# A fused attention and two mixture-of-experts kernel: ranks' products four turns later, last logits inside the first expert's products

## The chip, the cores and the metric

The kernel runs on one core of one Trainium2 chip. Times are device microseconds of one execution, lower is better. Three runs of the kernel before took 864.76, 865.23 and 867.83 us; their median, 865.23 us, is the time before.

## What is computed

Three stages follow each other, all in float32. First attention of 4 batches, 8 heads, 576 positions and head size 64, where half of the heads look at the last 32 positions and half at every fourth of the last 128. Its output, 2304 rows of 512 numbers, goes through a mixture of 8 experts with the two best experts per row, and that result through a second mixture with the best expert alone.

```python
x = attn_out.transpose(0, 2, 1, 3).reshape(B * S, H * D)
logits = x @ w_gate
noisy_logits = logits + np.log1p(np.exp(x @ w_noise)) * noise
top2 = np.argpartition(-noisy_logits, 2, axis=1)[:, :2]
...
h = np.maximum(x[mask] @ w1[e], 0.0)
out[mask] += top2_w[mask, k, None] * (h @ w2[e])
```

## The kernel before

**Attention in turns.** The attention works on 36 banks, nine blocks of 64 positions in each of four batches. One pass of the loop over `i` is one turn for one bank: scores of the next bank, softmax of this one, transposes of the exponentials `pe` of an older one (`t` and `q`), its product with the values (`v`), and for the oldest the transposes of its output `xo` (`x`), after which the rows go to memory. Three more passes, `i` = 36 to 38, empty the pipeline. The letters `a`, `v`, `w`, `t`, `q`, `x` and `r` are PSUM banks, one of each and two of `a`. Almost every matmul goes through the helper `in_order`, at L237, which stamps it so that TensorE runs them in the order in which the program is written; so nearly every TensorE row carries the same line.

**Products in three passes.** Experts' weights and inputs are split in a high and a low part (`whi` and `wlo`, `xh` and `xl`, `hh` and `hl`); each product is three matmuls: high by high, low by high, high by low. A first product of an expert makes hidden rows, a second product output rows. ScalarE makes `whi` (L219), `xh` (L722) and `hh` (L777), VectorE `wlo` (L220), `xl` (L723) and `hl` (L778).

**Routing in small steps.** As soon as rows of attention output are there, `logits_part` (L1024) multiplies half a batch's transposed rows `xT` by the gate, VectorE copies the result to `lgT` (L702), and `batch_logits` (L1031) sums four parts of it and starts a routing chain. A chain is a generator; `go_on` (L1068) is one tick and lets each list of chains make two steps, four from turn 30 on. `yield n` in a chain means that it rests n ticks. The chain finds the two best experts, sums the one-hots to `msum` (L480, 481), and `ranks` counts with TensorE how many earlier rows go to each expert (`r<-msum,before` and `r<-msum,onesb`). From the ranks come slots and one-hots `ohb` on VectorE, `rhs` on POOL, further `r` products, and a table `tabe` with the list of rows of each expert. `indices` (L450 to L456) turns a piece of the table into a list for gathering (`gata`), and POOL gathers the rows (`xg`, L716). Three parts of the rows go through it: nine tiles of 128 rows (batches 0 and 1), which fix the 256 rows of the first expert; four more tiles (batch 2), which fix 384 rows of the second; and the last five (batch 3). `V2PE`, 2, and `PE2V`, 1, are the ticks that a chain rests between VectorE and TensorE.

**Around the end of attention.** From turn 35 on each pass ends with eight steps of the first expert's first products (`first_products`, three matmuls a step, `E0_N` = 8, in two calls of `DC` = 4, each with a tick behind it). When the last bank is finished, `finish` (L961) gives `ready` the two halves of the last batch, and after the loop their logits are computed. Then the second products of the first expert, the first and second of the second, and so on follow. `put_rows` (L1186) adds finished rows `y` (made by ScalarE, L1215) to the result in memory from POOL's queue.

Of the kernel before, what the change touches and what calls it, by code (L numbers as in the profile page):

```python
# [42 lines left out]
A2V, V2PE, PE2V, POOL2V = 4, 2, 1, 10  # L43
# [4 lines left out]
E0_AT, E0_N, E0_M = 35, 8, 1  # L48
# [16 lines left out]
def attention_moe_moe_kernel(  # L65
# [9 lines left out]
    E, _, F = m1_w1.shape  # L75
    HH = H // 2
    T = N // P
    DC = DM // P
# [27 lines left out]
    def bank(tag):  # L106
        return banks_of[tag].tile([P, 512], F32, name=tag)
# [125 lines left out]
    ordered = [False]  # L233

    def in_order(op, *args, **kw):

        r = op(*args, **kw)  # L237
        if ordered[0]:
            tc.stamp_issue_order_token(r.ins, "blocks")
        return r  # L240


    def rtile(shape, name, dt=F32):
        return rt.tile(shape, dt, name=name)
# [214 lines left out]
    class Route:  # L459
# [14 lines left out]
        def ranks(self, oh, weights, t0, t1):  # L474
            n = t1 - t0
            m = rtile([P, n + 1, E], "msum", BF16)
            if self.K == 1:
                nc.vector.tensor_copy(m[:, :n], oh[:, 0])
            else:
                nc.vector.tensor_add(m[:, :n], oh[:, 0], oh[:, 1])  # L480
            nc.vector.memset(m[:, n:], 0.0)
            val = yield from weights
            ps = bank("r")[:, :(n + 1) * E].rearrange("p (t e) -> p t e", e=E)
            in_order(nc.tensor.matmul, ps, before, m, start=True, stop=False)
            for i in range(n):
                in_order(nc.tensor.matmul, ps[:, i + 1:], onesb, m[:, i:i + 1, :].to_broadcast([P, n - i, E]),
                         start=False, stop=(i == n - 1))
            yield PE2V
            rk = rtile([P, n + 1, E], "rk")
            if self.prev is None:  # L490
                nc.vector.tensor_copy(rk, ps)
            else:
                nc.vector.tensor_add(rk, ps, self.prev[:, None, :].to_broadcast([P, n + 1, E]))
            cnt = rt.tile([P, E], F32, name="cnt", bufs=2)
            nc.vector.tensor_copy(cnt, rk[:, n])
            yield
            return val, m, rk, cnt
# [198 lines left out]
    def logits_T(xt, lgT, n, tag):  # L696

        lg = bank(tag)[:, :n]
        for c in range(DC):
            o = c * P // DC  # L700
            in_order(nc.tensor.matmul, lg[o:o + P // DC], wg1[:, c], xt[c], start=True, stop=True)
        nc.vector.tensor_copy(lgT, lg)  # L702
# [52 lines left out]
    def mm1_steps(ws, x_, n):  # L755
        xh, xl = x_
        up = -(-n // P) * P
        pool = pools["h", up == regs1[0][1]]
        hh = pool.tile([P, FC, up], F32R, name=f"hh{up}")
        hl = pool.tile([P, FC, up], F32R, name=f"hl{up}")  # L760
        m = n - up + P
        if m <= P // 2:

            last = hl[:, :, up - P:].rearrange("p f (a t) -> p f a t", a=2)
            if m < P // 2:
                nc.gpsimd.memset(last[:, :, :, m:].bitcast(F32), 0.0)
        for f in range(FC):
            ph = next_bank("avaw")
            i = 0
            for c in range(DC):  # L770
                wc = tuple(w_[:, f * P:(f + 1) * P] for w_ in ws[c])
                for a, b_ in passes(wc, (xh[:, c], xl[:, c])):
                    in_order(nc.tensor.matmul, ph[:, :n], a, b_[:, :n], start=(i == 0), stop=(i == 3 * DC - 1))
                    i += 1
                if c < DC - 1:
                    yield
            nc.scalar.activation(hh[:, f, :n], ph[:, :n], AF.Relu)  # L777
            nc.vector.scalar_tensor_tensor(hl[:, f, :n], ph[:, :n], 0.0, hh[:, f, :n].bitcast(F32),  # L778
                                           op0=ALU.max, op1=ALU.subtract)
            yield  # L780
        if m <= P // 2:
            nc.gpsimd.tensor_copy(last[:, :, 1, :m], hh[:, :, n - m:n].bitcast(F32))
        return hh, hl
# [23 lines left out]
    with ExitStack() as actx:  # L807
# [63 lines left out]
        def banks():  # L871

            for j in range(0, NB - 1, 2):
                for half in (1, 0):
                    yield (half, j), (half, j + 1)
            yield (0, NB - 1), (1, NB - 1)
# [25 lines left out]
        def scores(bk, bk_next):  # L902

            if bk_next is not None:
                open_scores(bk_next)
            for u in range(HH // 2):
                for a in range(2):
                    product(bk, a, HH // 2 + u)
                    if bk_next is not None:
                        product(bk_next, a, u)  # L910
# [113 lines left out]
        def logits_part(b, c0, n, xT, lgT):  # L1024
            o = b % 2 * S + c0

            logits_T([xT[:, c, c0:c0 + n] for c in range(DC)], lgT[:, o:o + n], n, "v" if c0 else "x")
            if c0 + n == S:
                backs.append((b, lgT))
# [24 lines left out]
        chains, ready, backs, routed, tick = ([], []), [], [], [0], [0]  # L1054
# [17 lines left out]
        def first_products(n):  # L1072
            if "h" not in nxt:
                nxt["h"] = Steps(mm1_steps(w_1, first_x[0], regs1[0][1]))
            nxt["h"].take(n)

        all_banks = [(b, bi, blocks) for b in range(B) for bi, blocks in enumerate(banks())]
        n_bi = len(all_banks) // B
        to_t, to_v, to_f = (sum(SKEW[:i + 1]) for i in range(3))
# [9 lines left out]
        for i in range(len(all_banks) + to_f):  # L1089
            bi = i % n_bi  # L1090
            if i >= LAST_AT:
                per_turn[0] = LAST_PER_TURN
                go_on()
            if i < len(all_banks):
                queue.insert(0, bks[i])
                scores(bks[i], bks[i + 1] if i + 1 < len(bks) else None)
                softmax(bks[i])
                if len(queue) > to_t and queue[to_t]:
                    transposes(queue[to_t])
                exponentials(bks[i])  # L1100
                if i < len(WARM_1):
                    busy(WARM_1[i], last_pe[0])
            else:
                queue.insert(0, None)
            if i >= len(all_banks) and len(queue) > to_t and queue[to_t]:
                transposes(queue[to_t])
            if len(queue) > to_v and queue[to_v]:
                values(queue[to_v])
            known_lg = bool(backs)
            while ready:  # L1110
                logits_part(*ready.pop())
            if len(queue) > to_f:
                bk = queue.pop()
                if bk.bi == 0:
                    xT = ak.tile([P, DC, S], F32, name="xT")
                    if bk.b % 2 == 0:
                        lgT = ak.tile([P, 2 * S], F32, name="lgT")
                bk.xT = xT
                finish(bk)
                if bk.bi == n_bi - 1:  # L1120
                    ready += [(bk.b, S // 2, S // 2, xT, lgT), (bk.b, 0, S // 2, xT, lgT)]
                if known_lg:

                    batch_logits(*backs.pop())
                    go_on()
            if i >= E0_AT and 0 in first_x:
                for _ in range(0, E0_N, DC):
                    first_products(DC)
                    go_on()

            if i < len(all_banks):
                if bi == 0:
                    more = [[] for _ in range(n_bi)]
                    b = i // n_bi + 1
                    if b < B:
                        next_b = b
                        more[0].append(load_k(b))
                        more[1].append(load_q(b))
                for c, (half, f) in enumerate(V_AT):

                    if f == bi and i // n_bi + 1 < B:
                        more[bi] += load_v(next_b, half, c // 2)
                if i in Z_AT:
                    z0 = Z_AT.index(i) * ZROWS
                    more[bi] += zeros(z0, min(ZROWS, N + P - z0))
                if last_st[0] is None:
                    issue(more[bi])
                else:
                    with tc.issue_after(last_st[0]):
                        issue(more[bi])  # L1150
            if i == W1_AT:
                with tc.issue_after(last_st[0]):
                    w_1 = load_w(wr1, m1_w1[0], F, nc.gpsimd, 4, None, nc.gpsimd)
# [435 lines left out]
```

## Time and profile before

| | before |
|---|---|
| Median of three runs | 865.23 us |
| The profiled execution | 860.84 us |
| Its span | 858.7 us |
| TensorE busy | 819.0 us (95%) |
| VectorE busy | 446.1 us (52%) |
| ScalarE busy | 380.1 us (44%) |
| POOL busy | 229.5 us (27%) |
| Mean granted TensorE clock | 0.979 |

The profile is of one execution; its own time, 860.84 us, is its span, from the first to the last instruction, and 2.1 us around it. The clock is the share of full speed that the chip granted: 1.00 is 2.4 GHz, 0.50 is 1.2 GHz. A bracket behind a row of a timeline gives how long the engine was idle before it and which instruction ended the idle time; "issue" there stands for nothing that the profile shows.

### The profile page before, as it was taken

What the parts mean: (1) busy time and instruction counts of PE and PEld (TensorE: products, weight loads), DVE (VectorE), ACT (ScalarE), POOL (GpSimd) and SP (SyncE); (2) the same over time, 40 slices, a digit from 0 to 9 for tenths busy, and PEclk for the clock granted to TensorE, in tenths of its full rate; (3) what the DMA queues carried; (4) which work ended last, traced back from release to release, by engine and by line L of the source; (5) the groups of instructions that cost most, each with busy time, mean ns of one, the idle gap of its engine ahead of it and who ended that gap; (6) DMA issues with size and microseconds to landing.
All of it is one profiled execution on the core that took longest, in us unless ns stands there. A gap on an engine that the chain in (4) does not pass through costs nothing. (4 is left out here: it accounts for less than half of the span.)

```text
span 858.7 us, 15516 instructions
## 1 busy us (share of the span) xinstructions
PE 819.0 (95%) x5798; PEld 701.9 (82%) x5798; DVE 446.1 (52%) x1255; ACT 380.1 (44%) x991; POOL 229.5 (27%) x290
## 2 busy tenths in 40 slices
PE   8998989999999999999999998998999999999994
PEld 6666677888898998898988987877878979889882
DVE  4677876874262146433515344574565556446450
ACT  3876554514263143433525244314415466446550
POOL 6062442032222232322323223313222121121111
PEclk9999889999999999999999999999999999999997
DMA  9989454453284436542814426445434656644530
GB/s 250 281 271 344 142 154 142 124 155 70 53 288 104 118 65 204 152 133 31 272 25 152 140 47 157 121 123 142 108 135 164 211 188 202 243 146 148 197 120 17
DMA packets 71919, 131.82 MB, mean 154 GB/s; under 512 B 5689, under 2 KB 34441, under 8 KB 71456
## 3 DMA queue, kind: packets, MB, share of 16 engines
q1 hardware_dynamic: 58640, 97.27, 34.5%
q0 software_dynamic: 13200, 33.52, 16.7%
q8 instruction: 47, 0.77, 0.4%
q14 instruction: 32, 0.26, 0.1%
HBM read 106.86 MB, written 24.15 MB: 153 GB/s over the span
## 5 line engine op out<-in xcount | busy, mean ns | idle before, releaser
L220 DVE TENSOR_TENSOR wlo<-raw,whi 128x512 fp32r<-128x512 f32 x264 | 165.4, 686 | 128.1 <-ACT whi L219 127.6
L219 ACT CAST whi<-raw 128x512 fp32r<-128x512 f32 x264 | 144.2, 618 | 49.0 <-DMA raw<-in_moe_w_dram 24.6
L237 PE MATMUL a<-xh,whi 128*128 128x256 f32 (+13 forms) x376 | 116.2, 309 | 0.1
L237 PE MATMUL a<-xh,wlo 128*128 128x256 f32 (+13 forms) x376 | 114.3, 304 | 2.1 <-issue 2.1
L237 PE MATMUL a<-xl,whi 128*128 128x256 f32 (+13 forms) x376 | 114.3, 304 | 1.4 <-DVE xl L723 1.4
L237 PE MATMUL a<-whi,hl 128*128 128x512 f32 (+4 forms) x248 | 98.0, 395 | 0.0
L237 PE MATMUL a<-wlo,hh 128*128 128x512 f32 (+5 forms) x248 | 97.5, 394 | 0.0
L237 PE MATMUL a<-whi,hh 128*128 128x512 f32 (+4 forms) x240 | 95.9, 399 | 0.8 <-ACT whi L219 0.8
L1186 POOL DMA_INDIRECT x_scratch<-y,sca x30 | 47.6, 1587 | 139.1 <-ACT y L1215 80.0
L778 DVE SCALAR_TENSOR_TENSOR hl<-a,hh 128x256 fp32r<-128x256 f32 (+13 forms) x94 | 43.5, 462 | 68.0 <-ACT hh L777 67.8
L777 ACT ACTIVATE hh<-a 128x256 fp32r<-128x256 f32 (+13 forms) x94 | 39.1, 416 | 81.3 <-PE a L237 81.2
L237 PEld LDWEIGHTS a<-xl,whi 128*128 128x128 f32 x376 | 72.4, 193 | 2.3 <-DVE xl L723 1.6
L237 PEld LDWEIGHTS a<-xh,wlo 128*128 128x128 f32 x376 | 72.3, 192 | 2.4 <-issue 2.4
L237 PEld LDWEIGHTS a<-xh,whi 128*128 128x128 f32 x376 | 72.5, 193 | 1.4 <-ACT xh L722 0.5
L716 POOL DMA_INDIRECT xg<-x_nextscratch,gat x30 | 34.9, 1164 | 85.5 <-PE t L237 25.4
L237 PE MATMUL w<-xh,whi 128*128 128x256 f32 (+13 forms) x184 | 56.4, 307 | 0.0
L237 PE MATMUL w<-xh,wlo 128*128 128x256 f32 (+13 forms) x184 | 55.5, 302 | 0.0
L237 PE MATMUL w<-xl,whi 128*128 128x256 f32 (+13 forms) x184 | 55.5, 302 | 0.0
L237 PEld LDWEIGHTS a<-whi,hl 128*128 128x128 f32 (+4 forms) x248 | 45.7, 184 | 11.2
L237 PEld LDWEIGHTS a<-wlo,hh 128*128 128x128 f32 (+5 forms) x248 | 45.2, 182 | 10.7 <-DVE wlo L220 0.5
L237 PE MATMUL v<-xh,whi 128*128 128x256 f32 (+13 forms) x176 | 53.4, 304 | 0.0
L237 PE MATMUL v<-xl,whi 128*128 128x256 f32 (+13 forms) x176 | 53.1, 302 | 0.1
(413 smaller groups left out, 1774.7 us busy)
## 6 DMA issues: line engine op xcount, KB each, us to landing
raw<-in_moe_w_dram SPq DMA_DIRECT2D x60, 1024.0 KB, 5.8
raw<-in_moe_w_dram SPq DMA_DIRECT2D x32, 256.0 KB, 5.2
v<-in_v_dram SPq DMA_DIRECT2D x16, 288.0 KB, 5.8
x_scratch<-zero SPq DMA_DIRECT2D x2, 1792.0 KB, 7.4
k<-in_k_dram SPq DMA_DIRECT2D x3, 1152.0 KB, 7.6
q<-in_q_dram SPq DMA_DIRECT2D x3, 1152.0 KB, 10.0
x_nextscratch<-xo SPq DMA_DIRECT2D x20, 128.0 KB, 4.6
x_scratch<-zero SPq DMA_DIRECT2D x1, 1280.0 KB, 5.1
```

Source lines behind the costliest of these rows:

```text
L219: nc.scalar.copy(hi_, raw_)
L220: (nc.vector if i % 2 == 0 and all_on is None else eng).tensor_sub(lo_, raw_, hi_.bitcast(F32))
L237: r = op(*args, **kw)
L716: last_g[0] = nc.gpsimd.indirect_dma_start(out=xg[:m], out_offset=None, in_=src, in_offset=bass.IndirectOffsetOnAxis(ap=idx[:m], axis=0)).ins
L777: nc.scalar.activation(hh[:, f, :n], ph[:, :n], AF.Relu)
L778: nc.vector.scalar_tensor_tensor(hl[:, f, :n], ph[:, :n], 0.0, hh[:, f, :n].bitcast(F32), op0=ALU.max, op1=ALU.subtract)
L1186: nc.gpsimd.indirect_dma_start(out=dst, out_offset=bass.IndirectOffsetOnAxis(ap=idx, axis=0), in_=y, in_offset=None, compute_op=ALU.add)
```

## The change

`Route.ranks` rests four ticks (`2 * V2PE`) more before its products, in the attention part of the program alone. At the last turn (`i` = 38) the first expert's first products are no longer eight steps in a row: four steps, the logits of one half, two steps, the logits of the other half, two steps.

```diff
@@ -480,6 +480,8 @@
                 nc.vector.tensor_add(m[:, :n], oh[:, 0], oh[:, 1])
             nc.vector.memset(m[:, n:], 0.0)
             val = yield from weights
+            if ordered[0] == "attention":
+                yield 2 * V2PE
             ps = bank("r")[:, :(n + 1) * E].rearrange("p (t e) -> p t e", e=E)
             in_order(nc.tensor.matmul, ps, before, m, start=True, stop=False)
             for i in range(n):
@@ -1124,8 +1126,17 @@
                     batch_logits(*backs.pop())
                     go_on()
             if i >= E0_AT and 0 in first_x:
-                for _ in range(0, E0_N, DC):
-                    first_products(DC)
+                for g in range(0, E0_N, DC):
+                    if i + 1 < len(all_banks) + to_f:
+                        first_products(DC)
+                    elif g == 0:
+                        first_products(DC)
+                        logits_part(*ready.pop())
+                    else:
+                        first_products(DC // 2)
+                        logits_part(*ready.pop())
+                        first_products(DC // 2)
                     go_on()
 
             if i < len(all_banks):
```

Line numbers behind L482 grow by 2, behind L1128 by 11. Three places show what moves.

TensorE, the ranks' products of the second part, before (`xo` is attention output, `msum` the summed one-hots, `xh_2141` the first expert's rows):

```order
L237 MATMUL t<-ident,pe 96x128 x2
L237 MATMUL q<-ident,pe 96x128 x2
L237 MATMUL v<-v,pT 64x64 x8
L237 MATMUL x<-ident,xo 128x128 x2
L237 LDWEIGHTS before
L237 MATMUL r<-msum,before 128x40
L237 LDWEIGHTS onesb
L237 MATMUL r<-msum,onesb 128x32
```

Here they follow the transposes `x` of one bank and precede the scores of the next. Now, from the same bank on:

```order
L237 MATMUL x<-ident,xo 128x128 x2
L237 MATMUL w<-k_273,q_271 64x96 x4
L237 MATMUL t<-ident,pe 96x128 x2
L237 MATMUL q<-ident,pe 96x128 x2
L237 MATMUL v<-v,pT 64x64 x8
L237 MATMUL x<-ident,xo 128x128 x2
L237 MATMUL a<-xh_2180,whi 128x256
```

The products are gone from behind the first `x`; they stand 24 first products later:

```order
L237 MATMUL a<-xh_2180,whi 128x256
L237 MATMUL a<-xl_2181,whi 128x256
L237 MATMUL a<-xh_2180,wlo 128x256
L237 LDWEIGHTS before
L237 MATMUL r<-msum,before 128x40
L237 LDWEIGHTS onesb
L237 MATMUL r<-msum,onesb 128x32
```

The first part's products move in the same way, from ahead of a bank's `v` to behind the next bank's scores.

TensorE at the end of attention, before, where the logits of the last two halves (`xT,wg`) come behind all first products:

```order
L237 MATMUL a<-xh_2141,whi 128x256
L237 MATMUL a<-xl_2142,whi 128x256
L237 MATMUL a<-xh_2141,wlo 128x256
L237 MATMUL x<-xT,wg_243 32x288 x4
L237 MATMUL v<-xT,wg_243 32x288 x4
L237 MATMUL v<-sum_245,lgT 128x16 x5
L237 MATMUL a<-whi,hh_2434 128x512
```

And now:

```order
L237 MATMUL a<-xl_2181,whi 128x256
L237 MATMUL a<-xh_2180,wlo 128x256
L237 MATMUL x<-xT,wg_243 32x288 x4
L237 MATMUL r<-rhs,ohb 128x120 x3
L237 MATMUL a<-xh_2180,whi 128x256
L237 MATMUL a<-xl_2181,whi 128x256
L237 MATMUL a<-xh_2180,wlo 128x256
L237 MATMUL a<-xh_2180,whi 128x256
L237 MATMUL a<-xl_2181,whi 128x256
L237 MATMUL a<-xh_2180,wlo 128x256
L237 MATMUL v<-xT,wg_243 32x288 x4
```

The first half's logits stand 12 first products ahead of the end, the second half's six. The last three `rhs` products of the second part, earlier well ahead of here, now stand among them.

POOL and TensorE at the end of the second expert's second products. POOL before (`gatf` and `gat` are lists of rows, `scaa` a list for adding):

```order
L716 DMA xg<-x_nextscratch,gatf 128x512
L716 DMA xg<-x_nextscratch,gatf 72x512
L716 DMA xg<-x_nextscratch,gat 128x512
L1186 DMA x_scratch<-y,scaa_2555 2432x512
L716 DMA xg<-x_nextscratch,gat 128x512
L716 DMA xg<-x_nextscratch,gat 104x512
```

And now:

```order
L718 DMA xg<-x_nextscratch,gatf 128x512
L718 DMA xg<-x_nextscratch,gatf 72x512
L1197 DMA x_scratch<-y,scaa_2650 2432x512
L718 DMA xg<-x_nextscratch,gat 128x512 x2
L1197 DMA x_scratch<-y,scaa_2650 2432x512
L718 DMA xg<-x_nextscratch,gat 104x512
```

The scatter has moved ahead of the first `gat`. TensorE before, at the transposes of these rows:

```order
L237 MATMUL t<-ident,xg 128x128 x4
L237 MATMUL a<-whi,hh_2902 128x512
L237 MATMUL a<-wlo,hh_2902 128x512
L237 MATMUL a<-whi,hl_2903 128x512
L237 MATMUL x<-ident,xg 128x72 x4
```

And now:

```order
L237 MATMUL a<-whi,hl_2903 128x512
L237 MATMUL t<-ident,xg 128x128 x4
L237 MATMUL x<-ident,xg 128x72 x4
L237 MATMUL q<-ident,xg 128x128 x4
L237 MATMUL v<-xh_3261,whi 128x200
```

A third transposition, `q`, stands between the second products and the first products of 200 rows; before, it stood behind these.

## Rows read from the trace of the kernel before

**Rows 1.** The page: engine, busy us, share of the span, instructions.

```profile
PE 819.0 (95%) x5798; PEld 701.9 (82%) x5798; DVE 446.1 (52%) x1255; ACT 380.1 (44%) x991; POOL 229.5 (27%) x290
```

**Rows 2.** Waits of TensorE: waited for, us in total, times, longest us.

```profile
PE r L237 <- DVE msum L481: 2.2, 1, 2.2
...
PE v L237 <- DVE xo L958: 1.8, 6, 0.5
```

**Rows 3.** TensorE's timeline: start, length, line, operation, count, idle before, releaser.

```profile
90.45 0.39 PE L237 MATMUL t<-ident,pe 128*96 128x128 f32 x2 [0.79 <-DVE ai L375]
...
92.28 1.10 PE L237 MATMUL v<-v,pT 96*64 96x64 f32 x16 [1.00 <-issue]
...
105.45 0.42 PE L237 MATMUL t<-ident,pe 128*96 128x128 f32 x2
```

**Rows 4.** Stretches: length; busy PE, PEld, DVE, ACT, POOL; PEclk, DMA share, GB/s.

```profile
92.00:96.00 4.00, 3.72 (x39) 2.90 (x40) 4.00 (x15) 1.85 (x10) 2.25 (x5) 0.54 0.18 49
96.00:100.00 4.00, 3.89 (x39) 2.23 (x39) 3.64 (x15) 1.66 (x9) 1.48 (x3) 0.60 0.92 347
...
116.00:120.00 4.00, 3.86 (x37) 3.04 (x38) 3.33 (x23) 3.04 (x17) 1.43 (x6) 0.53 0.84 242
120.00:124.00 4.00, 4.00 (x24) 4.00 (x24) 2.79 (x13) 1.39 (x7) 1.77 (x4) 0.62 0.73 207
...
140.00:144.00 4.00, 3.89 (x9) 2.81 (x10) 3.85 (x7) 3.81 (x9) 0.00 (x0) 0.57 0.10 16
152.00:156.00 4.00, 2.93 (x14) 1.90 (x12) 4.00 (x9) 3.19 (x6) 0.50 (x1) 1.00 0.69 179
...
588.00:592.00 4.00, 1.41 (x10) 0.93 (x10) 4.00 (x8) 4.00 (x9) 1.38 (x1) 1.00 0.59 158
```

**Rows 5.** TensorE's timeline, ranks' products of the second part.

```profile
116.14 0.19 PE L237 MATMUL r<-msum,before 128*128 128x40 bf16 x1 [2.24 <-DVE msum L481]
```

**Rows 6.** TensorE's timeline, end of attention and the first expert.

```profile
138.04 1.29 PE L237 MATMUL v<-sum,lgT 128*128 128x16 f32 x10 [0.58 <-DVE lgT L702]
140.08 0.78 PE L237 MATMUL a<-whi,hh 128*128 128x512 f32 x1 [0.75 <-ACT whi L219]
...
156.38 0.44 PE L237 MATMUL a<-xl,whi 128*128 128x384 f32 x1 [1.38 <-DVE xl L723]
```

**Rows 7.** VectorE's timeline, 115 to 156 us.

```profile
115.88 0.19 DVE L480 TENSOR_TENSOR msum<-oh 128x32 bf16<-128x32 f32 x1
...
130.22 0.27 DVE L553 TENSOR_TENSOR tabe<-tabe,r 128x120 f32<-128x120 f32 x1
...
140.15 4.91 DVE L220 TENSOR_TENSOR wlo<-raw,whi 128x512 fp32r<-128x512 f32 x8 [0.17 <-ACT whi L219]
...
155.64 0.69 DVE L723 TENSOR_TENSOR xl<-q,xh 128x512 fp32r<-128x512 f32 x1
```

**Rows 8.** TensorE's timeline, 168 to 192 us.

```profile
168.80 0.20 PE L237 MATMUL r<-msum,before 128*128 128x48 bf16 x1
...
189.45 0.66 PE L237 MATMUL t<-ident,xg 128*128 128x128 f32 x4
...
191.64 0.26 PE L237 MATMUL v<-xh,whi 128*128 128x200 f32 x1
```

**Rows 9.** POOL's timeline, 184 to 191 us.

```profile
184.78 1.01 POOL L716 DMA_INDIRECT xg<-x_nextscratch,gatf  x1 [1.24 <-DVE tabr L657]
...
187.42 0.98 POOL L716 DMA_INDIRECT xg<-x_nextscratch,gat  x1 [0.35 <-issue]
189.10 1.62 POOL L1186 DMA_INDIRECT x_scratch<-y,scaa  x1 [0.70 <-issue]
```

**Rows 10.** Tile `xg` (gathered rows), 100 to 206 us: landing of its transfers.

```profile
DMA to landing us min/median/max: 3.3/3.8/4.6
```

**Rows 11.** ScalarE's timeline: the row that the scatter takes.

```profile
185.59 0.69 ACT L1215 ACTIVATE y<-w,wgta 128x512 f32<-128x512 f32 x1 [5.98 <-PE w L237]
```

## The prediction

> **What bounds the kernel now.** I read the page's engine table first [rows 1]: TensorE is busy for 819.0 of 858.7 us and VectorE for 446.1. The end of the program is therefore set by TensorE, and what an edit is worth is the idle time of TensorE that it removes or adds, with the work that runs at half clock beside it. The table of waits then shows where that idle time is [rows 2]. The longest single wait that the diff touches is that of the ranks' products for `msum` (2.2 us, once); the waits of bank v for `xo` are six, of at most 0.5 us each. The timeline and the table by stretches give the places. They are three, all within the first 140 us.
>
> - Place A, where the first part of the tokens (nine tiles, for the first expert's list) is ranked: TensorE sits idle for 0.79 and 1.00 us [rows 3], and afterwards the granted clock is 0.54 and 0.60 for 8 us [rows 4], which is the lower of its two levels, 1.2 GHz, for most of them. VectorE is busy in these 8 us for 4.00 and 3.64, so it sets the pace too.
> - Place B, the ranks of the second part (four tiles, for the second expert's list): 2.24 us of waiting for `msum` [rows 5], then again 8 us at 0.53 and 0.62 [rows 4].
> - The end of attention, with the last logits: 0.58 us for the logits' copy `lgT`, 0.75 us for the first `whi` of the second products [rows 6], then a clock of 0.57 [rows 4].
>
> **The change, part by part.** No engine gets or loses work of any size: instructions change places. The first edit delays the ranks' products of two parts by four ticks, with all that follows from them: rank copies, slots, one-hots, rhs, table, gathers, and by these the first and second expert's transposes. The second edit moves the `xT,wg` products of the two halves of the last logits ahead of the last 12 and the last 6 first products, and the two `lgT` copies on VectorE with them.
>
> *Place A.* The first idle ended with a VectorE row of the slots' chain (`ai`), and for the second the profile names no releaser [rows 3]. I take both for VectorE: it works through slots and one-hots there, and the attention's `pe` and `xo` wait in its queue. Four turns later the same VectorE work stands ahead of the `xo` of a later bank. I lay out VectorE's rows in the new order and get two idles of about 0.8 and 0.95 us around 98 to 101 us: an estimate, of the size of the two in rows 3. So the stall moves and the clock falls as before: 0 us. Bounds: it could be 1.3 us better, if the clock stays up (TensorE reaches the transposes that now start at 105.45 [rows 3] at about 104.1 by the same layout; VectorE's load of 7.64 us in 8 [rows 4] keeps it from being more), and 1.0 us worse, if the fall comes where less VectorE work hides it.
>
> *Place B.* The wait of 2.24 us [rows 5] goes: `msum` is ready long before the products now. But TensorE then runs at once into products whose bank v still waits for the `xo` behind the top-two chain. That chain (on VectorE, ending with `msum` at 115.88 [rows 7]) waits for the noisy logits of POOL and does not move. My layout gives waits of 1.05 and 0.55 us there, and one of 1.0 us near 123 us behind the slots' chain: 2.6 in place of 2.24, a loss of 0.4. What may be gained is the clock. In the 8 us behind the old wait, 0.47 x 4 + 0.38 x 4 = 3.4 us of full-speed work were lost [rows 4]. With single waits of at most 1.05 us I take it that the clock stays: before 156.38 TensorE waited 1.38 us [rows 6], and behind 588 us it had only 1.41 us of work in 4 us, with a clock of 1.00 [rows 4]. Net -3.0 us. Bounds: -3.0 and +0.4 (clock falls all the same).
>
> Against that stands a rule of the Trainium skill, page "TensorE: Matmul & The Clock Gate", section "A second HAM failure mode: psum-queue depth-cycling": when TensorE pauses shortly and often between groups of products because it cycles through result banks, the clock goes back and forth, and each return is paid again. By it each of the new waits for bank v would cost the clock; rows 3 with 4 bear it out (0.79 and 1.00 us were enough), rows 6 and the stretch behind 588 us do not. It is the last rival below.
>
> *The end of attention.* The logits' products are the same, now between first products, and their copies too are covered: the 0.58 us go [rows 6]. The 0.75 us for ScalarE's `whi` stay: -0.6 us, bounds 0 and -0.6, since nothing new stands in that queue.
>
> *What is late next: the second expert.* The list of the second part (`tabe`, `gata`, `emp` and on to `prev`; eight small VectorE instructions from 130.22 on [rows 7], some 1 us of busy time) used to run before the last logits. It now stands between the `wlo` of the first expert's second weights, and the gathers follow it. The stretch from the first `wlo` at 140.15 to the `xl` at 155.64 [rows 7] is VectorE's, nearly without a gap: 4.00 of 4 us busy at 152 [rows 4]. So its list lengthens it by 1.0 us, and TensorE, which already waits for that `xl` (1.38 us [rows 6]), waits 2.4. +1.0; bounds 0, if TensorE's own work covers it, and 1.0.
>
> *And the third gather.* Its chain starts from the ranks at 168.80 [rows 8], which now stand six products later. Today the second products end with transposes of two gathered tiles, the first at 189.45, and the first products of 200 rows start at 191.64. In the new order a third transposition, of the tile that the first `gat` fetches, stands ahead of these 200-row products, and on POOL that gather stands behind the scatter, not ahead of it. POOL's gathers start at 184.78 and 187.42, the scatter takes 1.62 us at 189.10 [rows 9], and data is there 3.3 to 4.6 us after the gather starts [rows 10]. With the scatter first, the gather starts at about 187.4 + 1.6 + 0.3 = 189.3 and lands at 192.6 to 193.9, which is 23.8 to 25.1 us behind the ranks at 168.80. The first products then start 0.3 us after that and 0.6 us of transposes, at 193.5 to 194.8 instead of 191.64. The transposition is not done again later (0.4 us back): a loss of 1.5 to 2.7 us; I take 2.4, near the slower landing: the gather begun at 184.78 [rows 9] was in use only at 189.45 [rows 8], 4.7 us later. The scatter itself will not wait, for its `y` was made by 186.28 [rows 11]. Lower bound 0: TensorE may reach this place that much later for another reason, as the three stretches at half clock show. The Trainium skill's page "DMA: Bandwidth & Descriptors", section "Anatomy of one DMA — SWDGE (gpsimd) path", gives for POOL's transfers 2.0 us plus bytes over 436 GB/s, an estimate of 2.6 us for the 256 KB of a gather; by it the loss would be some 1 us less. The rows say 3.3 to 4.6.
>
> Behind this both orders are the same, row for row, and TensorE is the bound, so the difference is carried to the end. **Sum:** 0 - 3.0 - 0.6 + 1.0 + 2.4 = -0.2 us. Against the profiled execution's own 860.84 us this is 860.6. The median of the runs shown is 865.23, 4.4 us above it, so the forecast is 865.0 us. About 0.5%, 4.3 us, is what a measurement of this kernel can tell from no change.
>
> **The rivals.**
>
> *1. The full gain.* Place A and B keep the clock, the gather lands in time, and TensorE's own work covers VectorE's list: -1.3 - 3.0 - 0.6 = -4.9, 860.3 us. For it: the waits for `msum` and `lgT` are simply gone, and no new wait at A or B is longer than the 1.38 us that cost nothing [rows 6]. Against it: VectorE is busy for 7.64 us of 8 at 92 us and for 4.00 of 4 at 152 us [rows 4].
>
> *2. The third gather.* TensorE stands idle before the 200-row products for 2.7 us, and the clock falls there, which costs 3.4 us by the stretch behind 116 us [rows 4]. With the 1.0 us of the list and B and the end as forecast: +3.5, 868.7 us. If the clock also falls at B: +6.9, 872.1 us. It decides where idle time and fall together are over the 3.6 us that B and the end give back. For it: 2.24 us of idle did this [rows 5]. Against it: the stretch behind 588 us, where 2.6 us of idle did not.
>
> *3. Nothing moves.* VectorE's chain, not the place of the products, sets the pace. A and B lose the clock as before, the gather lands in time: +0.4 - 0.6 + 0 = about 0, 865.2 us. VectorE's 7.64 of 8 us at A speaks for it; its 3.33 us in the 4 behind 116 us [rows 4], which leave a gap at B, speak against it.
>
> *4. Many small waits.* Every new wait costs the clock, as 0.79 and 1.00 us did at A [rows 3, 4]. This is what the rule named above would make of it. A 0, B +0.4, end -0.6, list +1.0, gather 2.4 with a fall of 3.4: +6.6, 871.8 us.
>
> **How the numbers follow.** Forecast 0.30, rival 1 0.17, rival 2 0.28, rival 3 0.15, rival 4 0.10. Faster by over 0.5%, below 860.9, is rival 1: 0.17. Slower by over 0.5%, above 869.6, is rival 4 and two thirds of rival 2: 0.28. The rest, 0.55, is within the bound. The range goes from rival 1 to rival 4 and the better part of rival 2: 860.3 to 871.9 us. It is wide because each of three places may or may not lose the clock, at 3.4 us each.
>
> **What would show it.** In the changed profile: no wait of `r` for `msum`, and none of `v` for `lgT`; the granted clock near 1.00 from 116 to 124 us; idle of about 0.8 to 1.0 us before bank v at 98 to 101 us and at 115 us; TensorE waiting some 2.4 us for `xl` before the first products of 384 rows; a wait of 1.5 to 2.7 us for the gathered tile before those of 200 rows. I would be wrong if the third gather makes no wait, if the second products of the first expert start less than 2 us or more than 6 us earlier than 140.08, or if the two profiles differ behind the 200-row products by more than at their start.

## The result and the profile after

The change takes 871.91 us in the median of 20 runs (867.42 to 877.69), the kernel before 865.19 us in 20 (860.27 to 869.59). The ratio is 1.0085 with a 95% interval of 1.0064 to 1.0106: slower by 7.4 us, 5.5 to 9.2. (Ratios are formed without disturbed runs, medians with all, so the two can differ by a few tenths of a per cent.) The profiled execution of the change took 871.08 us with a span of 869.0 us, 10.3 us more than the span before, because the profiled execution before was a quick one (860.84 against its median of 865.19).

TensorE's waits in the changed kernel (waited for, us in total, times, longest us) have a new first row.

```profile
PE q L237 <- DMA xg<-x_nextscratch,gat: 4.5, 1, 4.5
PE v L237 <- DVE xo L960: 4.4, 7, 1.7
...
PE a L237 <- DVE xl L725: 1.4, 2, 1.2
...
PE a L237 <- ACT xh L724: 1.2, 1, 1.2
...
PE a L237 <- ACT whi L219: 0.8, 1, 0.8
```

The wait for `msum` is gone [rows 2], and so is the one for `lgT`. In their place stand seven waits for `xo` of 4.4 us together, where there were six of 1.8, a wait for `xh` ahead of the second expert's products, and 4.5 us for one gathered tile. The `whi` wait of 0.75 us stayed, as expected.

The table by stretches of the changed kernel (length; busy PE, PEld, DVE, ACT, POOL; PEclk, DMA share, GB/s) shows where the clock was lost.

```profile
96.00:100.00 4.00, 2.39 (x31) 1.35 (x31) 3.46 (x14) 1.52 (x7) 1.87 (x4) 0.93 0.82 300
100.00:104.00 4.00, 4.00 (x31) 3.63 (x30) 1.99 (x10) 2.03 (x10) 1.08 (x3) 0.50 0.06 17
104.00:108.00 4.00, 4.00 (x31) 3.43 (x32) 1.15 (x4) 0.00 (x0) 0.00 (x0) 0.50 0.05 15
108.00:112.00 4.00, 4.00 (x41) 2.77 (x40) 2.31 (x13) 2.43 (x13) 2.10 (x2) 0.50 0.20 41
112.00:116.00 4.00, 4.00 (x53) 2.93 (x53) 2.23 (x7) 2.56 (x12) 1.97 (x8) 0.86 0.45 138
116.00:120.00 4.00, 3.35 (x53) 2.61 (x50) 3.34 (x15) 2.72 (x13) 1.38 (x6) 1.00 0.54 164
120.00:124.00 4.00, 3.80 (x37) 3.38 (x35) 2.95 (x15) 2.52 (x13) 0.24 (x1) 1.00 0.90 263
140.00:144.00 4.00, 3.73 (x9) 2.77 (x10) 3.98 (x15) 3.64 (x7) 2.50 (x2) 0.57 0.18 47
156.00:160.00 4.00, 2.77 (x9) 2.53 (x9) 3.15 (x12) 1.61 (x4) 1.59 (x1) 0.69 0.91 267
...
196.00:200.00 4.00, 1.23 (x6) 1.23 (x7) 0.00 (x0) 0.08 (x1) 2.20 (x3) 0.81 0.53 152
200.00:204.00 4.00, 4.00 (x21) 4.00 (x21) 1.06 (x2) 0.85 (x2) 1.90 (x2) 0.50 0.89 175
```

Before, the clock fell at 92 us and again at 116 us [rows 4]. Now it stays at 1.00 from 116 to 124 us, but it falls late in the stretch from 96 us and does not come back before the one from 112 us. The clock lost in the two old stretches and in this one is the same: (0.46 + 0.40 + 0.47 + 0.38) x 4 = 6.8 us before, (0.07 + 3 x 0.50 + 0.14) x 4 = 6.8 us now. New are the falls in the stretches from 156 and from 196 us.

TensorE's timeline at the attention and at the two experts (start, length, operation, idle before and releaser), answering to [rows 3, 5, 6, 8]:

```profile
92.85 0.39 PE L237 MATMUL t<-ident,pe 128*96 128x128 f32 x2 [0.73 <-DVE pT L942]
...
97.47 0.69 PE L237 MATMUL v<-xT,wg 128*32 128x288 f32 x8 [1.66 <-DVE xo L960]
```

```profile
123.30 0.19 PE L237 MATMUL r<-msum,before 128*128 128x40 bf16 x1
...
140.04 0.50 PE L237 MATMUL a<-whi,hh 128*128 128x512 f32 x1 [0.75 <-ACT whi L219]
...
155.80 0.44 PE L237 MATMUL a<-xh,whi 128*128 128x384 f32 x1 [1.23 <-ACT xh L724]
157.47 0.69 PE L237 MATMUL a<-xl,whi 128*128 128x384 f32 x1 [1.24 <-DVE xl L725]
```

```profile
172.50 0.20 PE L237 MATMUL r<-msum,before 128*128 128x48 bf16 x1
...
193.41 0.60 PE L237 MATMUL t<-ident,xg 128*128 128x128 f32 x4
...
198.77 1.11 PE L237 MATMUL q<-ident,xg 128*128 128x128 f32 x4 [4.50 <-DMA xg<-x_nextscratch,gat]
199.54 0.52 PE L237 MATMUL v<-xh,whi 128*128 128x200 f32 x1
```

The ranks' products of the second part now start at 123.30 without a wait, and the first expert's second products start at 140.04 where it was 140.08. From there on time is lost. The 384-row products wait twice, and the third transposition waits 4.50 us ahead of the 200-row products, which start at 199.54 instead of 191.64. POOL's timeline shows why:

```profile
182.54 1.58 POOL L1197 DMA_INDIRECT x_scratch<-y,scaa  x1 [0.86 <-ACT y L1226]
...
187.98 1.01 POOL L718 DMA_INDIRECT xg<-x_nextscratch,gatf  x1 [1.22 <-DVE tabr L659]
189.31 0.97 POOL L718 DMA_INDIRECT xg<-x_nextscratch,gatf  x1 [0.31 <-issue]
192.27 1.63 POOL L1197 DMA_INDIRECT x_scratch<-y,scaa  x1 [2.00 <-DMA x_scratch<-y,scaa]
194.21 1.02 POOL L718 DMA_INDIRECT xg<-x_nextscratch,gat  x1 [0.31 <-PE t L237]
```

The scatter did not start when POOL was free, at 190.28, nor when its `y` was there (188.91 by ScalarE's row below), but 2.00 us later, and the profile puts this wait down to the scatter before it, issued at 182.54, which had to land first. The gather behind it in POOL's queue started at 194.21 and its rows were used at 198.77.

```profile
188.22 0.69 ACT L1226 ACTIVATE y<-w,wgta 128x512 f32<-128x512 f32 x1 [5.96 <-PE w L237]
```

The kernel before has the same slow scatter, and there it cost nothing. POOL's timeline before has its start, and the view of its tile from 179 to 182 us its landing, 8.5 us later, at 188.4 us:

```profile
179.88 1.57 POOL L1186 DMA_INDIRECT x_scratch<-y,scaa  x1 [1.43 <-ACT y L1215]
```

```profile
DMA to landing us min/median/max: 8.5/8.5/8.5
```

The next scatter started at 189.10 [rows 9], but the third gather stood ahead of it on POOL and was on its way from 187.42.

The table cuts the way to the start of the 360-row products, from where both kernels run the same program, into three stretches. The bounds are the starts of the first expert's second products, of the second expert's `xl,whi` products and of the 360-row products; the last three columns are lengths.

| us | first expert's second products start | to the 384-row `xl` product | to the 360-row products | 360-row products start |
|---|---|---|---|---|
| before | 140.08 | 16.30 | 59.40 | 215.78 |
| the change | 140.04 | 17.43 | 68.22 | 225.69 |

So of 9.9 us in this pair of profiles, nothing is lost ahead of the first expert's second products, 1.1 us from there to the second expert's `xl` product and 8.8 us behind it. The last 8.8 us hold the wait of 4.50 us and two falls of the clock: 1.7 us lost behind the waits for `xh` and `xl`, 3.4 us behind the wait for the gather. The rest of the program adds 0.4 us.

### The profile page after: what moved, and what is told of

The parts are those of the page before. It is cut to its first block, busy times and chain, and to the rows that moved or that the text cites. A ratio compares the mean times of both kernels' runs of the same rounds, so it can differ in the third digit from the quotient of the medians.

```text
span 869.0 us, 15519 instructions
## 1 busy us (share of the span) xinstructions
PE 824.8 (95%) x5798; PEld 707.9 (81%) x5798; DVE 444.8 (51%) x1255; ACT 379.7 (44%) x991; POOL 231.2 (27%) x290
## 5 line engine op out<-in xcount | busy, mean ns | idle before, releaser
L237 PE MATMUL v<-xh,wlo 128*128 128x256 f32 (+13 forms) x176 | 53.6, 305 | 0.0
```

## The experiments

Theory: the loss is made at the end of the second expert, by two changes of order together: TensorE transposes the third gathered tile ahead of the 200-row products, and POOL starts its gather behind a scatter that waits. I call it the tail. In the first four runs the theory named TensorE's order alone; POOL's came in with the next four, and that both are needed with the last three. The rivals were that the logits cost, that the loss is made at the head (delay, late list and half clock at the attention's end), or that TensorE's order alone makes the tail's loss. Each run was timed in five rounds beside the kernel before on the same chip; ratios are to that. The kernels of a paragraph ran together.

**First four runs.** The ranks' delay alone, which is the change without its second part:

```diff
             val = yield from weights
+            if ordered[0] == "attention":
+                yield 2 * V2PE
             ps = bank("r")
```

> The ranks' delay alone, with the logits where they were. Theory (tail): nearly all of the loss comes from the third gathered tile's transposes, which stand ahead of the first products of 200 rows; they still do here, so 870.5 to 873 us, with a wait of 4 to 5 us for that gather and a half-clock stretch behind it. Rival (logits): moving the logits is what costs, so 865 to 867 us here.

Measured: 870.16 us, 1.0091 (1.0055 to 1.0127); by time just under the forecast, on a chip where the kernel before took 862.98. The delay alone makes the whole loss. Its table of TensorE's waits holds the same row:

```profile
PE q L237 <- DMA xg<-x_nextscratch,gat: 4.1, 1, 4.1
```

The moved logits alone (the second part of the diff without the first):

> The moved logits alone. Theory (tail): the end of the second expert's second products keeps the old order, so 864 to 866 us, at most the 0.6 us of the lgT wait better than before. Rival (logits): 868 us or more.

Measured: 864.78 us, 1.0009 (0.9975 to 1.0043), no difference. The rival of the logits falls.

The whole change with TensorE's order at the tail restored. The 200-row products and the next transposes are stamped for the order of the program:

```diff
             else:
+                ordered[0] = si == 1
                 h = mm1_unit(w1, x0 if ui == 0 else xs[ui].result, n)
...
                     if si > 0:
                         x_next.take(99)
+                        ordered[0] = False
```

> The whole change, but the first products of 200 rows keep their place ahead of the third gathered tile's transposes. Theory (tail): the wait of 4.5 us and its clock fall go, 5 to 7 us less than the change: 865 to 867 us. Rival (head): what is lost is lost earlier, at the attention's end and at the second expert's list (4.0 us in the profiles), and the wait is only moved: 870 to 872 us.

Measured: 869.16 us, 1.0076 (1.0049 to 1.0103), between the two forecasts. The change itself was not on this chip; the delay alone was, and the pinned kernel is only 1.0 us quicker than that, where the theory expected 5 to 7 us less than the change. It was repeated below.

The delay for the second part alone (`ordered[0] == "attention" and t0 > 0`):

> The delay for the second part's ranks alone, with the moved logits. The end of the second expert keeps the old order. Theory (tail): no loss, and without the delay of the first part the two idles at 90 and 92 us are as before while the 2.24 us wait for msum goes: 862 to 866 us. Rival (head): the second part's late list costs by itself: 867 to 870 us.

Measured: 865.30 us, 1.0004 (0.9967 to 1.0040). The end of the second expert has the old order and there is no loss. But nothing is gained either. The wait for `msum` was only replaced: TensorE's timeline has one of 2.65 us for `xo` and one of 2.25 us for `pe`.

```profile
99.37 1.19 PE L237 MATMUL v<-xT,wg 128*32 128x288 f32 x8 [2.65 <-DVE xo L960]
...
122.67 0.77 PE L237 MATMUL t<-ident,pe 128*96 128x128 f32 x2 [2.25 <-ACT pe L931]
```

**The next four.** The change again, and beside it the pinned kernel again:

> The change once more, beside the next three on one chip. Both theories: 1.007 to 1.010 of before, with one wait of 4 to 5 us for the third gathered tile.

Measured: 869.49 us, 1.0070 (1.0038 to 1.0101), with a wait of 4.24 us for the third tile.

> The change with the first products of 200 rows kept ahead of the third gathered tile's transposes, beside the change on the same chip. Theory (tail): 3.5 to 6 us less than the change; what stays above before (1 to 3 us) is the half-clock stretch behind the second expert's late rows. Rival (head): within 1.5 us of the change, since the stretch at half clock at the attention's end makes the loss.

Measured: 866.09 us, 1.0033 (0.9992 to 1.0075), 3.4 us less than the change beside it, just under what the theory expected (3.5 to 6). By this pair about half of the loss goes with the place on TensorE; by the first pinned run hardly any did. In its profile, TensorE's timeline first, the 200-row products start 1.77 us behind the first transposition, while in POOL's the scatter is still first and still waits:

```profile
195.80 0.60 PE L237 MATMUL t<-ident,xg 128*128 128x128 f32 x4
...
197.57 0.36 PE L237 MATMUL v<-xh,whi 128*128 128x200 f32 x1 [0.91 <-ACT xh L724]
```

```profile
194.88 1.63 POOL L1197 DMA_INDIRECT x_scratch<-y,scaa  x1 [2.23 <-DMA x_scratch<-y,scaa]
196.82 1.02 POOL L718 DMA_INDIRECT xg<-x_nextscratch,gat  x1 [0.31 <-PE x L237]
```

The reverse, the kernel before with the third transposition ahead of the 200-row products (the tile behind it is gathered earlier too):

```diff
             else:
+                if si == 1 and ui == 1:
+                    ordered[0] = True
+                    x_early = Steps(seg_x(segs[2], 0))
+                    x_early.take(2)
                 h = mm1_unit(w1, x0 if ui == 0 else xs[ui].result, n)
...
-                    x_next = Steps(seg_x(segs[si + 1], 0))
+                    x_next = x_early if si == 1 else Steps(seg_x(segs[si + 1], 0))
                     if si > 0:
                         x_next.take(99)
+                        ordered[0] = False
```

> The kernel before with the third gathered tile transposed ahead of the first products of 200 rows; on POOL its gather still starts ahead of the scatter. Theory (scatter order): the gather lands in time or nearly so, a wait under 2.5 us and no lasting loss: 1.000 to 1.003 of before. Rival (place on TensorE alone): a wait of 4 us or more and a clock fall as in the change: 1.006 or more.

Measured: 865.34 us, 1.0029 (0.9991 to 1.0067). The interval holds both 1.000 and 1.006, so the time alone does not decide. The trace does. TensorE does not wait at `q` at all, because its gather starts ahead of the scatter; the scatter waits behind it, where nobody needs it. TensorE's timeline, then POOL's:

```profile
189.16 0.64 PE L237 MATMUL t<-ident,xg 128*128 128x128 f32 x4
...
191.34 0.60 PE L237 MATMUL q<-ident,xg 128*128 128x128 f32 x4
191.69 0.34 PE L237 MATMUL v<-xh,whi 128*128 128x200 f32 x1
```

```profile
187.16 0.98 POOL L716 DMA_INDIRECT xg<-x_nextscratch,gat  x1 [0.34 <-issue]
188.90 1.62 POOL L1186 DMA_INDIRECT x_scratch<-y,scaa  x1 [0.75 <-DMA x_scratch<-y,scaa]
```

Two ticks of delay instead of four (`yield V2PE`):

> The change with two ticks of delay in place of four; the end of the second expert then has the old order on TensorE and POOL. Theory (tail): 0.997 to 1.003 of before. Rival (the delay itself costs, by its length): half of the loss, 1.004 to 1.005.

Measured: 866.89 us, 1.0022 (0.9989 to 1.0054). It has the old order at the tail and most of the loss is gone. The interval also holds the rival's 1.004 to 1.005, so a cost of the delay itself is neither shown nor excluded by the time. The waits at the head were only exchanged here too, as TensorE's timeline shows:

```profile
99.97 1.08 PE L237 MATMUL v<-xT,wg 128*32 128x288 f32 x8 [1.82 <-DVE xo L960]
...
123.50 0.71 PE L237 MATMUL v<-v,pT 96*64 96x64 f32 x16 [2.19 <-issue]
```

**The last three.** The change with one thing else, on POOL. The scatters of the second and third output tile are held back until the third tile's gather is issued; TensorE still transposes the third tile ahead of the 200-row products:

```diff
+    held_rows, hold = [], [False]
+
     def put_rows(y, idx, accumulate, dst):
+        if hold[0]:
+            held_rows.append((y, idx, accumulate, dst))
+            return
...
+                    x_early = Steps(seg_x(segs[2], 0))
+                    x_early.take(1)
+                    with tc.issue_after(last_g[0]):
+                        while held_rows:
+                            put_rows(*held_rows.pop(0))
+                    x_early.take(1)
```

> The change with one thing else on POOL: the gather of the third tile starts ahead of the scatter of the second expert's second output tile, as in the kernel before. TensorE keeps the order of the change, third transposes first. Theory (both orders needed): the wait of 4 to 5 us for the gathered tile falls under 1.5 us and no clock fall follows it; 3 to 6 us less than the change on the same chip. Rival (place on TensorE): the wait stays over 3 us and the time within 1.5 us of the change.

Measured: 866.71 us, 1.0017 (0.9982 to 1.0052). The change itself on the same chip:

> The change itself beside the other two on one chip: 1.007 to 1.010 of before in both theories.

Measured: 869.20 us, 1.0070 (1.0043 to 1.0096), with the same row in its table of TensorE's waits:

```profile
PE q L237 <- DMA xg<-x_nextscratch,gat: 4.4, 1, 4.4
```

So 0.5% by the ratios, 2.5 us by the medians, goes with POOL's order alone. The forecast was 3 to 6 us: 0.5% is 4.6 us, the medians fall short of it. With the gather first, POOL starts it at 189.56 and the scatter follows; TensorE's only waits in this place are 0.47 us for ScalarE and 0.43 us for `xl` behind it. POOL's timeline, then TensorE's:

```profile
189.56 0.98 POOL L718 DMA_INDIRECT xg<-x_nextscratch,gat  x1 [0.36 <-issue]
191.41 1.62 POOL L1202 DMA_INDIRECT x_scratch<-y,scaa  x1 [0.87 <-issue]
```

```profile
192.35 0.60 PE L237 MATMUL t<-ident,xg 128*128 128x128 f32 x4
...
193.04 0.60 PE L237 MATMUL q<-ident,xg 128*128 128x128 f32 x4
194.11 0.36 PE L237 MATMUL v<-xh,whi 128*128 128x200 f32 x1 [0.47 <-ACT xh L724]
```

The delay for the first part alone (`and t0 == 0`):

> The delay for the first part's ranks alone, with the moved logits; the end of the second expert keeps the old order. Theory (tail): 0.997 to 1.003 of before, with a fall of the clock between 96 and 104 us in place of the one at 92. Rival (head): this delay brings the long half-clock stretch at the attention's end and costs by itself: 1.004 or more.

Measured: 866.29 us, 1.0029 (0.9996 to 1.0062). No loss that can be told from none, though the interval holds the rival's 1.004 too. The half clock of the attention's end is there, and with the first pinned profile's it is the longest. The table by stretches (PEclk is the third number from the right):

```profile
96.00:100.00 4.00, 3.39 (x31) 1.84 (x31) 2.70 (x11) 0.62 (x1) 1.48 (x3) 0.63 0.57 204
100.00:104.00 4.00, 4.00 (x31) 3.77 (x30) 1.76 (x8) 2.03 (x10) 1.09 (x3) 0.50 0.10 27
...
112.00:116.00 4.00, 4.00 (x39) 2.73 (x38) 1.74 (x7) 2.03 (x10) 2.06 (x8) 0.50 0.42 125
116.00:120.00 4.00, 3.98 (x41) 3.25 (x42) 2.77 (x11) 2.52 (x11) 1.30 (x5) 0.81 0.48 145
```

Put together, the tail is a two by two. The number is the stretch from the second expert's `xl` product to the 360-row products, in us; the same kernel has 59.40 before.

| | POOL: gather first | POOL: scatter first |
|---|---|---|
| TensorE: 200-row products first | 59.40 (before), 59.48 (logits alone), 59.44 (second part), 60.92 (first part), 61.41 (two ticks) | 62.28 and 62.25 (pinned) |
| TensorE: third transposes first | 58.96 (before, transposes first), 60.27 (the change, gather first) | 68.22, 64.95 and 67.37 (the change), 66.26 (delay alone) |

Six of these stretches hold a fall of the clock at the second expert's late rows. It begins over 20 us ahead of the scatters and does not belong to the two orders. In the runs of the first part, of two ticks and of both pinned kernels, and in the change's 68.22, it loses 1.7 us; in the change's 67.37 it loses 2.6 us. With this taken off, the stretch is 59.2 to 59.7 us where both orders are old, 59.0 to 60.6 where one is new (at most 1.2 us more than before), and 64.8 to 66.5 where both are new (5.4 to 7.1 us more). The pinned pair's 1.2 us are the waits for `xh` and `xl` of the 200 rows.

By these profiles the head does not make the loss. In the seven profiles with the delay of both parts in full, the first expert's second products start at 137.87 to 142.49 us, 140.0 in the mean; in the three without a delay at 139.60 to 140.63. They start late in the three runs with part of the delay (142.52, 145.27 and 146.63 us), whose times show no clear loss.

## Why the prediction was wrong, step by step

The forecast was 865.0 us, no change, and it came out 871.9. Rival 2, the third gather with a fall of the clock, was the mechanism, with 868.7 to 872.1 us and a chance of 0.28. Two of the signs of being wrong came: the first expert's second products start 0.04 us earlier, not 2 to 6, and the profiles differ by 7.9 us at the 200-row products and by 9.9 us behind them.

- **Place A**, taken as 0: the two idles stand at 92.85 and 97.47 us, not at 98 to 101, as 0.73 and 1.66 us instead of 0.8 and 0.95, and the clock fell behind the second of them, until 113 us.
- **Place B**, taken as -3.0: the wait for `msum` and the fall of the clock behind it are gone as forecast. In this profile they did not come back as gain, for the clock lost at A grew by as much: together with the end of attention, -3.6 was forecast and 0.0 measured. In the two other profiles of the change A loses only 1.7 us, B none, and the second products start at 137.87 and 138.05, 2.2 and 2.0 us earlier; the waits for `xo` are 5.1 and 5.9 us in all there, 1.8 before.
- **The second expert's list**, taken as +1.0: 17.43 against 16.30 us, +1.1. Right. That the clock then falls, by some 1.7 us at 156 us, I had given to no case; one of the two other profiles of the change has such a fall too, and one has not.
- **The third gather**, taken as +2.4: this is the step that failed. The sum named the wait and its cause rightly but missed its size. It said of the scatter that it "will not wait, for its `y` was made by 186.28". The profile shows it waiting 2.00 us for the scatter before it to land, and the trace before showed a start at 189.10, 2.8 us after the `y` [rows 9]. With that start the forecast's own sum gives 189.1 + 1.6 + 0.3 = 191.0 us for the gather, 1.7 us later than taken, and a loss of 3.2 to 4.4 us. In the change the gather then took 4.56 us from its start to its use (194.21 to 198.77), at the late end of the 3.3 to 4.6 us of [rows 10], and the ranks themselves stood six products later, 1.05 us, which I named and did not add. That gives 4.50 us of waiting instead of 1.5 to 2.7, and the clock fell behind it (3.4 us lost here, 1.7 in the two other profiles), which only rivals 2 and 4 held.
- **Rival 1** fell by the head and by the tail. **Rival 3** was half right in this profile, where A and B together lost as much clock as before; in the two other profiles they lost less, and the gather did not land in time.
- **Rival 4**, the Trainium skill's "TensorE: Matmul & The Clock Gate", section "A second HAM failure mode: psum-queue depth-cycling": at B the waits of 0.35, 0.30 and 0.88 us for gathered rows and bank v cost no clock (1.00 from 116 us to 132 us), so short pauses alone did not make it swing here. The falls stand behind 1.66, 1.23 with 1.24, and 4.50 us. One stands at 140 us behind 0.75 us alone, where 0.58 us preceded it before [rows 6]; but in the last of the three profiles of the change the same 0.75 us, at 138.05, cost none. So the rule is neither shown nor excluded here. That this rival's 871.8 us lies at the result is chance: its wait was 2.4 us, and at B it had a fall that did not come.
- The Trainium skill's "DMA: Bandwidth & Descriptors", section "Anatomy of one DMA — SWDGE (gpsimd) path": its fit gave an estimate of 2.6 us for this gather, the trace 4.56 us from start to use.

Shown by the runs is that the delay of both parts together makes the loss, that the logits do nothing, that the tail is long only where both orders are new, and that POOL's order restored removes most of the loss (1.0017 beside 1.0070 on one chip). TensorE's order restored removes the wait in both its profiles; in time it was 1.0033 beside 1.0070 on one chip, but 1.0076 in its first run, so how much of the time it gives back is known less well. Open is what stays in the kernels with a repaired tail, 0.2 to 0.3% where the intervals hold 1.000, and why the half clock at A lasts as long as it does.

## What to carry to other kernels

The delay in this chain of small steps was paid where the chain ends, not where it was put in. Follow such a delay to the last engine that must wait for it, and see whether the order of the queues there is still the same. On a queue that runs in order, ask of each transfer what it waits for, and not only when its data is there: here a scatter that adds to memory waited for the scatter before it, and took a gather with it. Such a wait can stand hidden in the trace before, behind work that the change moves. A gain from a clock that does not fall is not safe to add up place by place: one of three profiles of the change lost at A what it won at B.

## What was not expected of the hardware

The scatter's wait: the one issued at 182.54 held the next until 192.27, 9.7 us later. Between 140 and 240 us in the kernel before, transfers of this kind landed after 4.3 us at least, 5.0 in the median and 8.5 at most, and the 8.5 us are those of the same scatter, at 179.88. Its successor started 9.2 us behind it, with the third gather in between, so the wait cost nothing. Why this one lands late is not shown. The DMA share of the two stretches from 180 to 188 us in the kernel before is 0.90 and 1.02, which may be the reason, but no run tests it.

And the length of a stretch at half clock. Twice the clock lost, which is the time at half clock, was 6.9 us at A before, 13.7 us in the change's first profile, 3.4 us in its two others, and 20.5 us in the run with the first part's delay alone and in the first pinned one. So the same program had 3.4 and 13.7 us. The mean granted clock goes with the time of a run: of the 35 runs of the kernel before beside the second four kernels, the four quickest (855.95 to 858.48 us) had 0.981 to 0.987, and three at 867.53 to 868.56 us had 0.967 to 0.969.
